# More idle products on TensorE in the front of a fused attention and gated-convolution kernel

## The chip, the cores and the metric

The kernel runs on one core of one Trainium2 chip. A core has five engines that run side by side and meet at semaphores: PE (TensorE, matrix products, with a separate row PEld for the loading of its stationary operand), DVE (VectorE), ACT (ScalarE), POOL (GpSimd) and SP (SyncE, which here only issues transfers). Sixteen DMA engines move data between the memory (HBM) and the core. Each engine works through its instructions strictly in the order in which they were written. The metric is the device time of one execution, in microseconds (us).

## What is computed

The reference is an attention over 8 batches, 12 heads, 448 positions and 64 elements a head, whose softmax has an additional 1 in its denominator, followed by a gated convolution that is done with Fourier transforms:

```python
# attention
scores = scale * np.matmul(q, k.transpose(0, 1, 3, 2))
m = np.max(scores, axis=-1, keepdims=True)
e = np.exp(scores - m)
attn = e / (np.sum(e, axis=-1, keepdims=True) + np.exp(-m) + 1e-09)
attn_out = np.matmul(attn, v)
x = attn_out.transpose(0, 2, 1, 3).reshape(B, S, H * D)
# gated convolution
x1, x2, x3 = split(x @ w_proj, 3)
x2_conv = irfft(rfft(x2, axis=1) * rfft(filter_fft, axis=0), axis=1)
out = (x1 * x2_conv * x3) @ w_out
```

All inputs and the output are float32; the kernel computes in bfloat16 with float32 sums.

## The kernel before

**Attention.** The 96 heads are handled in 48 pairs, six to a batch. For the first two batches (`staged`), k, q and v of each pair are loaded by SP's queue into a staging buffer (L398, L403), cast to bfloat16, nearly all by POOL (k in L425, q in L431, v in L438), turned by PE transposes (L465 and L467 for k, L474 for q, L499 for one piece of the first pair), and copied out of PSUM by DVE or ACT (L482 to L495, L502). For the later batches (`loaded`) the turning is done by DMA transposes on SP's queue (L542, L547). A pair's scores are products of `kT` and `qT` (L773 for three tiles of keys with two heads each, L775 for the shared rest of the keys), the exponentials run on ACT (L780, L786), the products with v on PE (L798, L806), and DVE divides by the sum: `rec` in L819 and L820, the result `xb` in L821. In the first two batches PE turns `xb` (L901), and DVE or ACT copies it to `xT` (L908, L910).

**Convolution.** For each batch DVE folds `xT` (L950, L953, L958), PE multiplies by the weights and by tables of sines (L981, L1011, L1049, L1095, L1134), ACT and DVE do the products between, and PE multiplies by `wout` (L1207); ACT copies the result out (L1219) and SP's queue stores it (L1226). Early on, PE also mirrors the table (L678), turns it (L692) and computes the filter's spectrum (L725, L728).

**The order.** All of it is written as tasks with an engine, an estimated cost and a wanted time. The class `Plan` plays them through on its own estimated clock: at each moment each engine takes the first of its waiting tasks, sorted by wanted time, that is ready. That gives one fixed order for each engine, and also the PSUM bank of each task; there are eight banks. The planned times are estimates and not those of the chip.

**Idle products.** Before any data is there, PE does 38 products of a tile of zeros with itself (`spin`, L1314). When the order is fixed, `fillers` (L232) goes through PE's tasks once more. Wherever there is a planned gap between the planned end of one task and the planned start of the next, and that end lies between the first two numbers of `FILL` (L60), it sets `count` products of the same kind (L1306) ahead of the next task, if `count` is at least 2 and some PSUM bank is unused throughout the planned gap. The third number of `FILL` is the share of the planned gap that `count` is to take, with 0.056 us counted for one product:

```python
if end is not None and self.FILL[0] <= end < self.FILL[1]:
    count = int(self.FILL[2] * (at - end) / 0.056)
```

Their results are never read. The product itself is 128x128 by 128x128 in bfloat16. Because an engine works in order, the task behind them can't start before they have been issued, however early its data is there. A bank that a preceding task used has to be read out first, so the first idle product can carry a wait for the engine that reads it.

Of the kernel before, what the change touches and what calls it, by code (L numbers as in the profile page):

```python
# [41 lines left out]
class Plan:  # L42
# [14 lines left out]

    NBANKS = 8
    LOW = 4
    FILL = (3.0, 36.0, 0.6)  # L60
    PAIRS = ("sc", "op")
    CAP = {"sc": 2, "op": 2, "hy": 5}

# [168 lines left out]
    def fillers(self, order, gone):  # L232
# [7 lines left out]
        for n, (at, t) in enumerate(order):  # L240
            if t[2] != "PE":
                continue
            if end is not None and self.FILL[0] <= end < self.FILL[1]:
                count = int(self.FILL[2] * (at - end) / 0.056)
                free = [
# [1144 lines left out]
```

## Time and profile before

| | |
|---|---|
| median of 4 runs | 382.97 us (382.32 to 384.26) |
| the profiled execution's own time | 382.79 us |
| its span, first to last instruction | 380.9 us |
| PE busy | 365.8 us (96%), 3681 products |
| DVE busy | 258.6 us (68%) |
| ACT busy | 262.1 us (69%) |
| POOL busy | 113.8 us (30%) |
| idle products L1306 | 90, from 5.0 to 34.7 us |
| mean granted clock of PE | 0.995 |

An engine's busy time counts its computing instructions. The granted clock is the share of full speed at which PE was allowed to run. The 40 digits of a row of slices stand for 9.5 us each. A line of the timeline has the start, the length, the engine, the line of the kernel, the operation with its tiles and shape, the number of instructions merged, and in brackets how long the engine had been idle and what ended the wait. Durations of products overlap, since PE is pipelined; the spacing of their starts tells how fast they went.

### The profile page before, as it was taken

How to read it: one execution, taken by the hardware profiler on the slowest of the kernel's cores; microseconds unless marked ns; L12 is line 12 of the kernel's file. 1: busy time of each engine (PE TensorE's matmuls, PEld its weight loads, DVE VectorE, ACT ScalarE, POOL GpSimd, SP SyncE). 2: the span in 40 equal slices, each digit the busy share in tenths (PEclk: the TensorE clock that was granted, in tenths of full speed). 3: DMA queues.
4: the chain of work that ended last, by engine and by line, in shares of the span. 5: the costliest groups of instructions: out<-in, count | busy, mean ns of one | idle time of the engine just before them, and what ended most of it. 6: DMA issues, size and time to landing. Idle time of an engine off the chain costs nothing.

```text
span 380.9 us, 9521 instructions
## 1 busy us (share of the span) xinstructions
PE 365.8 (96%) x3681; PEld 224.6 (59%) x3681; DVE 258.6 (68%) x672; ACT 262.1 (69%) x456; POOL 113.8 (30%) x232
## 2 busy tenths in 40 slices
PE   8887999999999999999999999999999999999994
PEld 7566765556655567555765555655555555655552
DVE  6496769945888548893489845694377936984770
ACT  6686876756886768877787846776778477544622
POOL 4795822422653635453362510000000000000000
PEclk9998999999999999999999999999999999999999
DMA  8999999989999999999999975932422034315205
GB/s 214 252 236 251 234 203 222 132 118 251 192 214 207 182 296 242 223 159 244 268 241 157 228 160 120 202 85 100 98 54 44 18 102 91 84 46 122 83 0 167
DMA packets 148653, 62.27 MB, mean 163 GB/s; under 512 B 113469, under 2 KB 145024, under 8 KB 148608
## 3 DMA queue, kind: packets, MB, share of 16 engines
q1 hardware_dynamic: 111184, 51.89, 61.3%
q0 software_dynamic: 37184, 9.54, 26.7%
q8 instruction: 29, 0.48, 0.5%
q10 hardware_dynamic: 240, 0.23, 0.2%
q14 instruction: 16, 0.13, 0.1%
HBM read 43.86 MB, written 11.01 MB: 144 GB/s over the span
## 4 chain that ended last, share of the span: by engine, by line
PE 66%; DMA 12%; DVE 10%; ACT 4%; POOL 3%; issue 3%; SPq 2%; ACTq 0%; POOLq 0%; DVEq 0%
PE psum L1095 21%; PE psum L1207 11%; PE psum L1011 7%; PE psum L806 6%; PE psum L773 6%; PE psum L981 5%; DMA nat<-in_k_dram 4%; DMA out_dram<-osb 2%; DMA rests<-in_v_dram 2%; PE psum L1049 2%; ACT e L780 2%; DMA nat<-in_q_dram 2%; PE psum L775 2%; DVE t L1063 1%; POOL vn L602 1%
## 5 line engine op out<-in xcount | busy, mean ns | idle before, releaser
L780 ACT ACTIVATE e<-psum 128x896 bf16<-128x896 f32 x144 | 125.6, 923 | 19.3 <-PE psum L773 18.5
L1095 PE MATMUL psum<-xT,wproj_bf 128*128 128x448 bf16 x576 | 121.1, 352 | 1.5 <-DVE g L1110 1.3
L1095 PEld LDWEIGHTS <-wproj_bf 128*128 128x128 bf16 x576 | 54.1, 97 | 46.3 <-issue 3.4
L1207 PE MATMUL psum<-wout_bf,yT 128*128 128x384 bf16 x288 | 51.8, 326 | 0.4 <-DVE g L1110 0.2
L1219 ACT COPY osb<-psum 128x384 f32<-128x384 f32 x56 | 26.0, 484 | 28.1 <-PE psum L1207 24.7
L806 PE MATMUL psum<-vn,e 128*128 128x65 bf16 x1152 | 44.7, 194 | 0.0
L1107 ACT CAST x<-psum 128x448 bf16<-128x448 f32 x48 | 25.8, 537 | 27.5 <-PE psum L1095 27.4
L773 PE MATMUL psum<-qT,kT 64*128 64x448 bf16 x288 | 41.7, 357 | 1.1 <-DVE xb L821 0.6
L1063 DVE TENSOR_TENSOR t<-xs,hrs 113x768 bf16<-113x768 bf16 (+1 forms) x64 | 34.8, 579 | 9.3 <-ACT xs L1057 9.0
L806 PEld LDWEIGHTS <-e 128*128 128x128 bf16 x1152 | 39.0, 98 | 2.7
L602 POOL CAST vn<-nat 128x192 bf16<-128x192 f32 x72 | 28.1, 418 | 41.1 <-DMA nat<-in_v_dram 26.4
L1207 PEld LDWEIGHTS <-yT 128*128 128x128 bf16 x288 | 27.7, 98 | 19.6 <-issue 1.4
L819 DVE TENSOR_SCALAR rec<-psum 128x8 f32<-128x8 f32 x48 | 7.8, 162 | 44.8 <-PE psum L806 39.2
L536 POOL DMA_DIRECT2D nat<-in_q_dram x28 | 24.9, 890 | 40.1 <-DMA qT<-nat 24.9
L1110 DVE TENSOR_TENSOR g<-x,psum 128x448 bf16<-128x448 bf16 x48 | 29.4, 615 | 10.5 <-PE psum L1095 9.9
L981 PE MATMUL psum<-wproj_bf,xf 128*113 128x384 bf16 x192 | 35.2, 327 | 0.0
L821 DVE TENSOR_TENSOR xb<-psum,rec 128x512 bf16<-128x512 f32 x48 | 33.2, 691 | 1.7
L1057 ACT CAST xs<-psum 113x384 bf16<-113x384 f32 (+1 forms) x64 | 27.5, 496 | 4.7 <-PE psum L1049 3.8
L1011 PE MATMUL psum<-xf,wproj_bf 128*128 128x452 bf16 x144 | 30.5, 356 | 0.0
L786 ACT ACTIVATE er<-psum 128x448 bf16<-128x448 f32 x48 | 26.7, 557 | 4.0 <-PE psum L775 4.0
L981 PEld LDWEIGHTS <-xf 128*113 128x113 bf16 x192 | 24.6, 132 | 6.6 <-issue 0.9
L1143 ACT CAST cr<-psum 128x452 bf16<-128x452 f32 x48 | 24.2, 556 | 3.5 <-PE psum L1134 3.5
(113 smaller groups left out, 459.9 us busy)
## 6 DMA issues: line engine op xcount, KB each, us to landing
nat<-in_k_dram SPq DMA_DIRECT2D x48, 192.0 KB, 5.5
nat<-in_v_dram SPq DMA_DIRECT2D x48, 192.0 KB, 5.3
out_dram<-osb SPq DMA_DIRECT2D x24, 384.0 KB, 3.3
nat<-in_q_dram POOLq DMA_DIRECT2D x20, 168.0 KB, 6.9
nat<-in_q_dram SPq DMA_DIRECT2D x11, 224.0 KB, 6.6
wproj_bf<-in_moe_w_proj_dram POOLq DMA_DIRECT2D x2, 1152.0 KB, 15.3
rests<-in_k_dram SPq DMA_DIRECT2D x8, 192.0 KB, 5.5
rests<-in_v_dram SPq DMA_DIRECT2D x8, 192.0 KB, 6.9
```

The costliest lines, as they stand in the source:

```text
L602: nc.gpsimd.tensor_copy(vn[b % 2][:, hp, 4 * u : 4 * u + 3, 0:DH], sv[:, u])
L773: nc.tensor.matmul(sc[:, u, 0:S], kT[b % 2][c, hp, t, :], qT[b % 2][c, hp, :])
L780: nc.scalar.activation(e[:, 0 : 2 * S].rearrange("p (u n) -> p u n", u=2), pair(("sc", ("S", i, t)))[:, :, 0:S], AF.Exp, scale=SCALE,)
L806: nc.tensor.matmul(out_bank(u)[:, n, :], P["e"][1 + t][:, u * S + n * 128 : u * S + n * 128 + 128], vn[b % 2][:, hp, 4 * u + t, :], start= ...
L821: nc.vector.tensor_tensor(W["xb", b][:, hp].rearrange("p n (u d) -> p u n d", u=2), op[:, :, :, 0:DH], rec[:].unsqueeze(3).to_broadcast([1 ...
L981: nc.tensor.matmul(pps[:FQ, :DCH], W["xf", b][:, pg, kt, 0:FQ], wproj_bf[:, kt, D + ch * DCH : D + (ch + 1) * DCH], start=(kt == 0), stop= ...
L1011: nc.tensor.matmul(pps[:, 0 : 4 * FQ], wproj_bf[:, kt, D + dt * 128 : D + (dt + 1) * 128], W["xf", b][:, :, kt, 0:FQ], start=(kt == 0), st ...
L1057: nc.scalar.copy(L["xs", par, ch][:K, pg % 2, :], L["Z", pg, ch][:K, :DCH])
L1063: nc.vector.tensor_tensor(t[:K], L["xs", par, ch][:K], h, op=ALU.mult)
L1095: nc.tensor.matmul(p[:, :S], wproj_bf[:, kt, 2 * part * D + dt * 128 : 2 * part * D + (dt + 1) * 128], xT()[:, kt, 0:S], start=(kt == 0), ...
L1110: nc.vector.tensor_tensor(g[:, dt, :], L["x1", dt], p[:, :S], op=ALU.mult)
L1207: nc.tensor.matmul(ops[:n, :DCH], y[:, dt, 0:n], wout_bf[:, dt, ch * DCH : (ch + 1) * DCH], start=(dt == 0), stop=(dt == NDT - 1),)
```

## The change

One line changes:

```diff
-    FILL = (3.0, 36.0, 0.6)
+    FILL = (3.0, 50.0, 0.9)
```

The idle products take nine tenths of a planned gap instead of six tenths, and planned gaps that begin up to 50 us on the planner's clock are considered instead of 36 us. The order of the tasks and their banks are decided before `fillers` runs and stay as they are. The products are zeros times zeros as before, and their results are still read by nothing.

## The prediction

> **What bounds the kernel now.** I read first the page, for when PE (TensorE) is busy and at what clock:
>
> ```profile
> PE   8887999999999999999999999999999999999994
> ...
> PEclk9998999999999999999999999999999999999999
> ```
>
> A slice is 9.5 us. PE is short of full only in the first four, and in the fourth its clock dips. After 38 us it is full nearly everywhere, so what counts is when PE comes out of the front. Whatever still delays it after its last free wait stands, at first sight, in the end time. Next I cut the front into stretches of 3.41 us that end where the clock changes (columns: stretch, length, busy us of each engine, granted clock, DMA):
>
> ```profile
> 8.37:11.79 3.42, 1.87 (x26) 1.41 (x25) 0.96 (x2) 2.04 (x3) 2.73 (x11) 1.00 1.12 264
> ...
> 28.85:32.26 3.41, 1.48 (x20) 0.93 (x17) 3.10 (x10) 1.42 (x3) 1.79 (x5) 1.00 1.15 241
> 32.26:35.68 3.42, 3.42 (x30) 2.64 (x29) 0.75 (x1) 2.41 (x6) 0.87 (x2) 0.50 1.21 241
> ```
>
> PE was busy 1.48 of 3.41 us, and exactly then the clock fell to 0.50 and stayed there for 3.42 us. In the first row PE was busy 1.87 us and the clock stayed at 1.00. So in this execution the border for keeping the clock lay somewhere between 1.48 and 1.87 busy us in such a stretch. Then the timeline of PE in the front (start, length, line, what, count, idle before and its releaser); L1306 are the idle products:
>
> ```profile
> 10.23 0.37 PE L474 MATMUL psum<-ident_bf,q 112*128 112x112 bf16 x4 [1.28 <-POOL q L431]
> 10.44 0.95 PE L1306 MATMUL psum<-idle 128*128 128x128 bf16 x14
> 11.65 0.36 PE L775 MATMUL psum<-qT,kT 128*128 128x448 bf16 x1 [0.27 <-DVE kT L484]
> ...
> 16.29 0.61 PE L1306 MATMUL psum<-idle 128*128 128x128 bf16 x8
> 16.74 0.35 PE L775 MATMUL psum<-qT,kT 128*128 128x448 bf16 x1
> ...
> 27.22 0.40 PE L901 MATMUL psum<-ident_bf,xb 128*128 128x128 bf16 x4 [1.14 <-DVE xb L821]
> ...
> 32.05 0.45 PE L901 MATMUL psum<-ident_bf,xb 128*128 128x128 bf16 x4 [1.93 <-DVE xb L821]
> 32.29 1.70 PE L1306 MATMUL psum<-idle 128*128 128x128 bf16 x14
> 33.78 0.58 PE L775 MATMUL psum<-qT,kT 128*128 128x448 bf16 x1
> 34.16 0.95 PE L1306 MATMUL psum<-idle 128*128 128x128 bf16 x7
> 35.04 0.84 PE L773 MATMUL psum<-qT,kT 64*128 64x448 bf16 x4
> ```
>
> One product's record is 0.22 us long at full clock and 0.31 at half. So 14 in 0.95 us are (0.95 - 0.22)/13 = 0.056 us apart, and 14 in 1.70 us (1.70 - 0.31)/13 = 0.107. The waits in brackets are the cushions of the front; the last are 1.14 us at 27.22 and 1.93 us at 32.05. Last I read the chain that ended last:
>
> ```profile
> 31.30 0.70 DVE xb L821
> ...
> 131.53 4.89 DMA out_dram<-osb
> ...
> 136.44 0.49 ACT osb L1219
> ```
>
> VectorE (DVE) ends both of PE's long waits (its xb at 31.30 is in the chain, the one at 26.47 too), and after 32.05 us PE, idle products included, is the chain. Much later, from 87 to 137 us, it runs through SP's queue and transfers.
>
> **The change part by part.** The built program has 145 idle products in the front instead of 90, 55 more; every other engine's order is unchanged. By place (time in the profile before, count before to after): 5.0 us 6 to 9; 5.7 us 2 to 3; 6.0 us 16 to 24; 7.5 us 2 to 4; 7.75 us 4 to 7; 8.5 us 0 to 2; 10.4 us 14 to 22; 16.3 us 8 to 12; 22.9 us 8 to 12; 23.8 us 0 to 2; 25.6 us 6 to 9; 29.8 us 3 to 5; 32.3 us 14 to 21; 34.2 us 7 to 11; 39.7 us 0 to 2. Only the last place comes from the longer front.
>
> - Up to 8.6 us: 19 more, 19 x 0.056 = 1.06 us. The next real work is the transpose at 10.23, which waits for POOL's cast of q, and that for a load; 1.28 us were idle there. The two products at 8.5 us newly wait for the exponential that frees their bank, which ended at 8.35 us and will end some 0.7 later, at 9.0; four transposes queued behind them then end near 9.8. Cost 0; with the cover gone it would be 1.06 us.
> - 10.4 us: 22 x 0.056 = 1.23, so they end at 11.67 where the scores L775 began at 11.65 behind a copy on DVE. Cost 0.02, gone in the 0.43 us that PE waits at 12.67 for POOL. Taken as 0.
> - 16.3 us: 4 x 0.056 = 0.22 us. The scores at 16.74 followed the products directly, and the products with v, L806, behind them end 0.22 later. DVE had idled 1.57 us until 18.47 for exactly those, and from there it works almost without a break to the two xb of the chain. So DVE hands 0.21 us to PE at 27.22 and 32.05. This is the one early group that isn't covered. Bounds 0 (DVE's small idle times take it) and 0.22; I take 0.21.
> - 22.9, 23.8 and 25.6 us: 9 more, 0.50 us, inside the 1.14 us before 27.22. Cost 0. 29.8 us: 2 more, 0.11, inside the 1.93 us. Cost 0.
> - 32.3 and 34.2 us: here no cushion is left, and the clock decides. The first product starts at 32.29 + 0.21 = 32.50. If the clock falls at 32.26 as before: 21 x 0.107 = 2.24, scores L775 at 34.74 (before: 33.78); 0.37 for them; from 35.11 five products at 0.107 up to 35.68, six at 0.056, and 0.07 to the scores L773: 36.05 (before: 35.04). These four now run at full clock, 0.39 us (12.97 to 13.36 in the timeline) in place of 0.68, so what follows starts at 36.44 against 35.72: +0.72. If the clock doesn't fall: 32.50 + 21 x 0.056 = 33.68; the copy of kT that L775 needs, ended by ACT at 33.55, comes 0.21 later; L775 at 33.82, products from 34.01, 11 x 0.056 + 0.07, L773 at 34.70, the next at 35.09: -0.63.
> - 39.7 us: 2 x 0.056 = 0.11, of which PE had about 0.09 free there (0.25 us between two steps that are 0.16 apart elsewhere); their bank is freed by ACT's L735, long done. +0.02, with 0.11 as the upper bound.
>
> Does the clock still fall? With two more products behind 30.0 us, and both ends 0.21 later, the idle stretch is 1.82 us in place of 1.93. Busy time in the stretch of 3.41 us before the fall goes from 1.48 to about 1.59, against the border between 1.48 and 1.87. It is nearer to the row that fell, so I take the fall as before.
>
> The Trainium skill, in "TensorE: Matmul & The Clock Gate" (Part 1 and the closing table), asks only that PE have no idle gap above about 3 us between bursts. The row differs: here the clock fell after 1.93 us of idleness. By the page no gap of this front needs products, the clock would hold with and without the change, and its cost would be that of the uncovered products alone: about +0.4, the 0.21 carried over and 4 x 0.056 at 34.2 us.
>
> **The sum.** +0.72 + 0.02 (and up to 0.1 more at the two changes of pace), taken as +0.8 on the profiled execution. That took 382.79 us (span 380.9, 1.9 around it), 0.18 below the median of the four runs, 382.97. 382.79 + 0.8 = 383.6.
>
> **The rivals.**
> 1. The clock stays full: -0.63 + 0.02 at 36 us. For it: 1.59 busy us isn't far from 1.87, and nothing shows that the stretches begin at the same moment in each run. Against it: 1.59 is nearer to 1.48. Not all of it reaches the end: at 136.97 PE waits 0.43 us for ACT, which waits for a store to land, in the chain through the transfers. If that is pinned, 0 is left; if it follows, -0.61; I take -0.4: 382.4.
> 2. Slower by more than 0.5%: the delay costs a place on SP's queue. The chain enters SP's queue at 87.67 behind an ACT copy that PE releases, so +0.8 enters with it; if a load or store then stands behind one DMA transpose more, that adds its issue, 1.88 us for the one at 128.23. 382.79 + 0.8 + 1.9 = 385.5. It decides once 1.1 us or more is added to the 0.8. For it: hardly any slack in that stage, POOL's casts of q waiting for PE at 37.41. Against it: the queues' order is fixed, and PE's own waits there are short.
> 3. Faster by more than 0.5%: the clock stays full and the stage from 87 to 137 us follows wholly, its waits at 114.37 (0.83) and 136.97 (0.43) going too: -0.61 - 1.26 = -1.9, 380.9. Against it: nothing in the change touches what these waits end on.
> 4. It does nothing: every extra product lies in idle time, 382.8. The lines after 32.05 speak against it, where the products are the chain.
>
> **How the numbers follow.** Half a per cent, 1.9 us, is about what a measurement of this kernel can tell from no change; the four runs alone reach from 382.32 to 384.26. Chances: the fall as before 0.40 (383.6, its own range 382.6 to 384.6); clock full 0.18 (382.4); nothing 0.05 (382.8); a place lost 0.25 (385.5); faster 0.12 (380.9). The first three are within half a per cent: 0.63. The range 381.0 to 385.8 leaves out half of the faster case and about a third of the slower.
>
> **What would show it.** Right: 145 products; PE's wait before 10.23 nearly gone; DVE's L819 at 18.47 later by 0.2; L901 at about 32.25; a granted clock of 0.5 behind it; 21 products 0.107 apart; the real work after L773 later by 0.7 to 0.9 us, kept to the end. Wrong: no fall of the clock (then 0.6 earlier at 36 us), a second fall elsewhere (up to half of 3.4 us), or a shift that grows between 87 and 137 us.

## The result and the profile after

The changed kernel takes 382.68 us (median of 43 executions, 380.27 to 391.67), the kernel before 384.05 us (64 executions, 381.80 to 388.39). The ratio is 0.9951, with a 95% interval from 0.9932 to 0.9970: half a per cent faster, just inside what I had called no change (0.5%), and in the opposite direction to my +0.2%. The ratio leaves out executions more than 1.5% above the fastest of their kernel, 12 of the 43 of the changed kernel (a group of their own, from 387.4 to 391.7 us) and 4 of the 64 of the kernel before, so it compares the lower group of the one with nearly all executions of the other; over all executions the two kernels have nearly the same mean, 384.29 and 384.50 us.

The profiled execution took 381.92 us with a span of 380.1 us (before 382.79 and 380.9). First the page's rows of slices of the changed kernel, PE's busy share and its granted clock, and the shares of the chain that ended last:

```profile
PE   8988999999999999999999999999999999999994
...
PEclk9998999999999999999999999999999999999998
...
PE 79%; DVE 11%; DMA 3%; ACT 2%; issue 1%; SPq 1%; POOL 1%; ACTq 0%; POOLq 0%; DVEq 0%
```

The last of these rows in the kernel before:

```profile
PE 66%; DMA 12%; DVE 10%; ACT 4%; POOL 3%; issue 3%; SPq 2%; ACTq 0%; POOLq 0%; DVEq 0%
```

The front is a little fuller, the dip of the clock in the fourth slice is still there, and transfers (DMA) have 3% of the chain, where they had 12% before. The stretches of 3.41 us on either side of the fall of the clock:

```profile
29.19:32.60 3.41, 1.59 (x22) 1.20 (x21) 2.54 (x10) 1.63 (x3) 1.22 (x4) 1.00 1.16 244
32.60:36.02 3.42, 3.42 (x31) 2.73 (x30) 1.84 (x2) 2.02 (x5) 2.04 (x3) 0.50 1.22 241
```

PE was busy 1.59 of 3.41 us, and the clock fell to 0.50 for 3.42 us, as forecast. PE's timeline in the front:

```profile
9.96 0.36 PE L474 MATMUL psum<-ident_bf,q 112*128 112x112 bf16 x4
10.15 1.39 PE L1306 MATMUL psum<-idle 128*128 128x128 bf16 x22
11.38 0.35 PE L775 MATMUL psum<-qT,kT 128*128 128x448 bf16 x1
...
15.39 0.83 PE L1306 MATMUL psum<-idle 128*128 128x128 bf16 x12
16.07 0.35 PE L775 MATMUL psum<-qT,kT 128*128 128x448 bf16 x1
...
19.49 0.37 PE L474 MATMUL psum<-ident_bf,q 112*128 112x112 bf16 x4 [0.98 <-POOL q L431]
...
31.82 0.40 PE L901 MATMUL psum<-ident_bf,xb 128*128 128x128 bf16 x4 [1.82 <-DVE xb L821]
32.05 1.94 PE L1306 MATMUL psum<-idle 128*128 128x128 bf16 x21
33.79 0.58 PE L775 MATMUL psum<-qT,kT 128*128 128x448 bf16 x1
34.16 1.38 PE L1306 MATMUL psum<-idle 128*128 128x128 bf16 x11
35.47 0.80 PE L773 MATMUL psum<-qT,kT 64*128 64x448 bf16 x4
36.11 0.28 PE L798 MATMUL psum<-vn,er 64*128 64x65 bf16 x8
```

The 55 additional products are all there, and the wait of 1.28 us in front of 10.23 is gone. The products with v (L798) that begin at 36.11 began at 35.72 before: PE is 0.39 us later here, and 0.41 us at 45 us. At the end it is 0.8 us *earlier*. So 1.2 us went between 45 us and the end. Most of it went at the two waits that rival 3 named. PE's timeline of the kernel before has them so, the second for a copy by ACT (L1219) whose own line follows:

```profile
114.37 1.29 PE L1095 MATMUL psum<-xT,wproj_bf 128*128 128x448 bf16 x6 [0.83 <-DVE g L1110]
...
136.97 0.35 PE L773 MATMUL psum<-qT,kT 64*128 64x448 bf16 x1 [0.43 <-ACT osb L1219]
```

```profile
136.44 0.48 ACT L1219 COPY osb<-psum 128x384 f32<-128x384 f32 x1 [1.64 <-DMA out_dram<-osb]
```

The same in the changed kernel:

```profile
114.09 1.29 PE L1095 MATMUL psum<-xT,wproj_bf 128*128 128x448 bf16 x6
...
134.65 1.14 PE L981 MATMUL psum<-wproj_bf,xf 128*113 128x384 bf16 x6
135.71 0.70 PE L773 MATMUL psum<-qT,kT 64*128 64x448 bf16 x4
```

```profile
135.54 0.48 ACT L1219 COPY osb<-psum 128x384 f32<-128x384 f32 x1 [1.01 <-DMA out_dram<-osb]
```

ACT's copy (L1219) still waits, 1.01 us instead of 1.64, for a store of an output tile to land, because the pool `otp` has three buffers and the copy needs the oldest. But PE's four scores at 135.71 run without a break, where before the fourth of them waited 0.43 us; and the wait of 0.83 us at 114.37 is gone too. PE gains 0.69 and 0.63 us at these two places; behind them it gains 0.71 more up to 200.82, where a wait of 0.56 us for DVE goes, and loses 0.84 from there to 206.98.

### The profile page after: what moved, and what is told of

The parts are those of the page before. It is cut to its first block, busy times and chain, and to the rows that moved or that the text cites. A ratio compares the mean times of both kernels' runs of the same rounds, so it can differ in the third digit from the quotient of the medians.

```text
span 380.1 us, 9631 instructions
## 1 busy us (share of the span) xinstructions
PE 367.9 (97%) x3736; PEld 227.9 (60%) x3736; DVE 257.8 (68%) x672; ACT 262.6 (69%) x456; POOL 112.0 (29%) x232
## 4 chain that ended last, share of the span: by engine, by line
PE 79%; DVE 11%; DMA 3%; ACT 2%; issue 1%; SPq 1%; POOL 1%; ACTq 0%; POOLq 0%; DVEq 0%
PE psum L1095 25%; PE psum L1207 14%; PE psum L806 8%; PE psum L981 8%; PE psum L1011 7%; PE psum L773 7%; PE psum L1049 2%; PE psum L775 2%; DMA rests<-in_v_dram 2%; PE psum L1134 2%; DVE g L1110 1%; DVE t L1063 1%; DMA nat<-in_q_dram 1%; DVE xf L958 1%; DVE xb L821 1%
## 5 line engine op out<-in xcount | busy, mean ns | idle before, releaser
L1219 ACT COPY osb<-psum 128x384 f32<-128x384 f32 x56 | 26.1, 484 | 27.1 <-PE psum L1207 25.7
L602 POOL CAST vn<-nat 128x192 bf16<-128x192 f32 x72 | 27.2, 407 | 37.4 <-DMA nat<-in_v_dram 27.4
```

Source lines behind the costliest of these rows:

```text
L602: nc.gpsimd.tensor_copy(vn[b % 2][:, hp, 4 * u : 4 * u + 3, 0:DH], sv[:, u])
```

## The experiments

In all of them, "later" and "earlier" are PE's moments in the profiled execution against the profile before, at the same instruction. The time "from 45 us to the end" is how much PE lost (+) or gained (-) behind 45 us of the profile before. Each median is of 12 executions if nothing else is said. The kernel before, run again on each occasion, had medians of 384.61, 384.42, 384.52, 385.22 and 384.64 us.

**Which group of products matters?** Four kernels leave out or keep one group of the products each. `FILL` takes several stretches for this:

```diff
-            if end is not None and self.FILL[0] <= end < self.FILL[1]:
-                count = int(self.FILL[2] * (at - end) / 0.056)
+            share = 0.0 if end is None else sum(s for a, z, s in self.FILL if a <= end < z)
+            if share:
+                count = int(share * (at - end) / 0.056)
```

No products at all behind the first 38:

```diff
-    FILL = (3.0, 36.0, 0.6)
+    FILL = ((3.0, 3.1, 0.0),)
```

> No idle products behind the first 38 (0 in place of 90). Clock theory (the products pay because they keep the granted clock from falling behind PE's waits): more falls of the clock between 8 and 40 us, each worth 0.7 to 1.7 us, so 1 to 4 us slower than before (0.3 to 1%). Cost theory (a product in front of work that is ready only delays it; this was the prediction's sum): the 21 products behind 32 us, 0.107 us each at half clock, go, up to 2 us faster at 36 us, less what the fall costs. Transfer theory (the products move the times at which casts free staging room, and the gain arises in the loads up to 140 us): PE leaves the front within 0.5 us of before, and the difference arises later.

Measured: ratio 0.999 (0.9946 to 1.0033), median 386.44 us (381.61 to 390.32), 6 of 12 executions above 386.5 us.

The larger share before a planned 16 us only:

```diff
-    FILL = (3.0, 36.0, 0.6)
+    FILL = ((3.0, 16.0, 0.9), (16.0, 36.0, 0.6))
```

> Nine tenths only in planned gaps that begin before 16 us (27 of the 55 added products, at 5 to 12 us), six tenths behind that. Clock theory: the clock held in this stretch in both profiles, so at most a small part of the change's gain, 0 to 0.7 us. Transfer theory: most of the change's gain of 1.9 us (0.5%), since the first scores and turns are what moved by a microsecond. Cost theory: no difference, the idle time before 10 us covers it.

Measured: 0.9984 (0.9949 to 1.0019), 384.14 us (381.06 to 386.37).

The larger share from a planned 30 us only:

```diff
-    FILL = (3.0, 36.0, 0.6)
+    FILL = ((3.0, 30.0, 0.6), (30.0, 50.0, 0.9))
```

> Nine tenths only in planned gaps that begin behind 30 us (15 of the 55: 3 to 5 at 30 us, 14 to 21 and 7 to 11 at 32 to 35, 0 to 2 at 40). Cost theory: 0.5 to 0.7 us slower than before. Clock theory: if the gain comes from the stretch where the profiles show the fall, most of 1.9 us faster, with the fall at 32 us gone in part of the executions. Transfer theory: 0.5 us slower, as by cost.

Measured: 0.9972 (0.9939 to 1.0005), 384.14 us (381.74 to 385.93).

The larger share up to a planned 31 us and no products behind it, so none where the clock falls:

```diff
-    FILL = (3.0, 36.0, 0.6)
+    FILL = ((3.0, 31.0, 0.9),)
```

> The change without its products behind 32 us: nine tenths up to planned 31 us, none from there on (32 fewer than the change at 32 to 35 us, 2 fewer at 40). Cost theory: PE leaves this place 1 to 1.4 us sooner than with the change, so about 1 us faster than it, 2.5 to 3 us (0.7%) faster than before. Clock theory: the time is that of the change or up to 1 us slower, since PE then idles in place of the products until its data comes and the clock may stay low for a second stretch of 3.4 us.

Measured: 0.9943 (0.9907 to 0.9979), 383.62 us (380.97 to 387.81).

No kernel of the four stands clearly apart from the others: the intervals overlap. What the profiles show is more useful. In the fourth, the scores at 33.16 are 1.88 us ahead of those of the kernel before at 35.04, as no product stands in front of them. But without these products PE is idle again, and the clock stays low for two stretches in a row:

```profile
28.57:31.98 3.41, 1.63 (x19) 0.90 (x16) 2.48 (x10) 1.74 (x3) 1.28 (x3) 1.00 1.16 258
31.98:35.40 3.42, 2.73 (x35) 1.82 (x36) 2.14 (x2) 3.39 (x7) 1.99 (x4) 0.50 1.22 235
35.40:38.80 3.40, 3.40 (x23) 2.67 (x21) 1.92 (x5) 1.38 (x4) 2.79 (x6) 0.50 1.15 281
```

At 45 us it is 0.34 us behind. From 32 us to there it lost 1.23 us and the changed kernel 0.63, so in these executions the products at 32 and 34 us earned more than they cost, with the clock back one stretch earlier. And all four profiles lose time where the changed kernel had gained it: from 45 us to the end +5.02, +3.70, +1.16 and +1.90 us. PE's wait for ACT's copy near 137 us is 3.57, 1.63, 1.30 and 2.49 us in them. The chain names the store behind it, with its issue and the time until it landed (131.53 and 4.89 in the profile before); in the first, the second and the third kernel:

```profile
133.94 7.05 DMA out_dram<-osb
```

```profile
132.14 4.98 DMA out_dram<-osb
```

```profile
132.62 4.89 DMA out_dram<-osb
```

So the wait has two sources: in the first kernel the store took 2.16 us longer to land, in the other two it took no longer than before but was issued 0.61 and 1.09 us later, with PE 0.50 us earlier and 0.22 us later than before at 134 us. My theory had no such term. New theory: the time is decided by how long ACT waits for the output buffer, and that has little to do with the products.

**Take that wait away.** A fourth output buffer; the order on each engine stays the same:

```diff
-    otp = ctx.enter_context(tc.tile_pool(name="otp", bufs=3))
+    otp = ctx.enter_context(tc.tile_pool(name="otp", bufs=4))
```

In the kernel before, twice:

> The kernel before with four output buffers osb in place of three; every engine's order is the same, so only ACT's wait for a store to land (which holds PE between 136 and 141 us, 0.4 to 3.6 us in the profiles so far) can go. Store theory (this wait is where executions differ, and the front's products move the end only through it): 1 to 2 us faster than before, executions closer together, and no clock fall near 140 us. Front theory (the end follows what the front does, the wait only passes it on): within 0.5 us of before. If 140 us is limited by the kT transposes on the same queue: the wait stays under another name, no gain.

> The kernel before with four output buffers again. Store theory: 0.996 of before again, no execution above 386.5.

Measured: 0.9962 (0.9933 to 0.9991), 383.17 us (381.53 to 385.53), and 0.9927 (0.9893 to 0.9961), 382.79 us (379.88 to 384.12).

In the changed kernel, twice:

> The changed kernel with four output buffers. Store theory: the same time as the kernel before with four buffers, within 0.4 us, plus the +0.4 us that PE is later at 36 us in the profile of the changed kernel. Front theory: still 1.5 to 2 us faster than the kernel before with four buffers.

> The changed kernel with four output buffers again. Store theory: within 0.6 us of the kernel before with four buffers on the same occasion, no execution above 386.5. If the front's products have a gain of their own: 1.5 to 2 us below it.

Measured: 0.9958 (0.9926 to 0.9990), 382.67 us (379.44 to 385.33), and 0.9966 (0.9933 to 1.0000), 382.99 us (380.44 to 385.99).

And with the fourth kernel above (no products behind a planned 31 us):

> Nine tenths up to planned 31 us, no products behind it, and four output buffers. In its profile without the fourth buffer PE was 1.9 us ahead of before at 35 to 110 us and waited 2.5 us at 139. Store theory: that lead comes through, 1.5 to 2 us faster than the kernel before with four buffers, 380 us. Front theory: as without the fourth buffer, 0.994 of before.

Measured: 0.9969 (0.9938 to 0.9999), 382.61 us (381.22 to 386.52). Here the expectation, 380 us, missed: it counted on a lead of PE from 35 to 110 us, but the lead at 33.16 us had turned into 0.34 us of lateness by 45 us, and with four buffers PE was 0.62 us late there.

With four buffers the kernel before and the changed one cannot be told apart: means of 24 executions each of 382.93 and 382.86 us, 0.07 apart. PE's wait for ACT's copy near 137 us is gone in every profile with four buffers; of the changed kernel's second run PE's timeline there reads:

```profile
134.52 0.55 PE L773 MATMUL psum<-qT,kT 64*128 64x448 bf16 x4
134.91 0.28 PE L798 MATMUL psum<-vn,er 64*128 64x65 bf16 x8
```

**How repeatable is the result itself?** The changed kernel and the kernel before, unchanged:

> The changed kernel again, beside the two kernels with four buffers. By the first measurement 0.995 of before (0.993 to 0.997). Store theory: the profile has either no wait at 137 us and a time near 381.5, or a wait of 2 us or more and a time above 384.

> The changed kernel a third time. If the change is really faster: 0.995 of before (0.993 to 0.997), as at first. If its share of executions with the long wait near 137 us differs from one occasion to the next: anything from 0.993 to 1.007, with executions near 381.5 and near 388.

> The kernel before, unchanged, measured as if it were another kernel: what this measurement makes of no change at all. Store theory (the end differs between executions of one kernel by the wait for a store near 137 us and a clock fall that follows it): a ratio anywhere from 0.995 to 1.005, as wide as the change's own. Front theory: 1.000 within 0.002.

Measured: the changed kernel 0.9996 (0.9944 to 1.0048), 387.09 us (380.62 to 390.33), and 1.0032 (0.9987 to 1.0078), 388.12 us (382.75 to 391.41); the kernel before 1.0006 (0.9972 to 1.0040), 384.85 us (383.33 to 387.57). The gain of half a per cent did not come back. Three occasions gave the same program 0.9951, 0.9996 and 1.0032, and in the last two 7 and 9 of 12 executions were above 386.5 us. Over all their executions the means of these two are 386.59 and 387.90 us, against 384.71 and 384.90 us of the kernel before on the same occasions. In its second profile the changed kernel waited 1.82 us near 137 us and took 386.14 us, just between the two cases expected of it. The ratio of the kernel before to itself, 1.0006, fits both expectations; what separates them is its profile.

The profile of the *unchanged* kernel shows what differs from one execution to the next. First ACT and PE near 136 us, then the store in the chain:

```profile
136.15 0.48 ACT L1219 COPY osb<-psum 128x384 f32<-128x384 f32 x1 [2.98 <-DMA out_dram<-osb]
```

```profile
136.68 0.35 PE L773 MATMUL psum<-qT,kT 64*128 64x448 bf16 x1 [1.78 <-ACT osb L1219]
```

```profile
129.35 6.77 DMA out_dram<-osb
```

Same program as the profile before, but the store took 6.77 us instead of 4.89 and PE waited 1.78 us instead of 0.43. What follows costs once more. The stretches of 3.41 us of this execution, first in the front, then around the wait:

```profile
28.43:31.84 3.41, 1.86 (x32) 1.31 (x29) 3.04 (x12) 1.78 (x3) 1.81 (x5) 1.00 1.16 262
31.84:35.26 3.42, 3.09 (x63) 2.49 (x61) 1.97 (x2) 3.19 (x7) 1.93 (x3) 1.00 1.21 233
...
134.26:137.67 3.41, 1.63 (x32) 1.04 (x32) 0.00 (x0) 1.52 (x3) 0.94 (x1) 1.00 1.16 382
137.67:141.08 3.41, 3.41 (x21) 2.43 (x18) 1.59 (x4) 1.49 (x3) 2.14 (x6) 0.50 1.20 316
```

In the front the clock did not fall here: the stretches begin elsewhere in this execution, the last one before 32 us held 1.86 busy us instead of 1.48, and PE was 1.54 us earlier at 36.8 us than in the profile before, 0.45 of it already at 32 us, with nothing in the program changed. At 137.67, after 1.63 busy us, it fell, which took PE from 0.30 us earlier (137.1 us) to 1.35 later (145 us). In the third execution of the changed kernel it is the same with larger numbers; its chain and PE's timeline:

```profile
132.70 8.40 DMA out_dram<-osb
141.12 0.49 ACT osb L1219
```

```profile
141.65 0.53 PE L773 MATMUL psum<-qT,kT 64*128 64x448 bf16 x1 [5.15 <-ACT osb L1219]
```

So one wait, for one store, makes 0 to 5.15 us in executions of one kernel, and the fall of the clock behind it up to 1.7 us more. With the fourth buffer no profile has either, and the upper group of times goes too: above 386.5 us were 28 of 67 executions of the changed kernel and 50 of 227 of the kernel before with three buffers, and 2 of 96 with four (shares of 0, 0.6, 0.9 and 1.2).

**How much lateness of the front reaches the end?** Four buffers, without products (twice), with twice the share, and with a share between:

```diff
-    FILL = (3.0, 36.0, 0.6)
+    FILL = (3.0, 50.0, 1.8)
```

> No idle products behind the first 38, with four output buffers. Without the fourth buffer PE was 1.5 us later than before at 45 us in its profile (the clock stood at 0.5 for 10 us of the front) and the end 6.5 later. Sum theory (what PE loses in the front reaches the end, the rest is the store): 1 to 2 us slower than the kernel before with four buffers, about 384.3, no execution above 387.5. If the transfers up to 140 us hold PE anyway: the same as the kernel before with four buffers, 382.9.

> No idle products behind the first 38, four output buffers, once more. Theory (carried to the end): whatever PE is late at 45 us in the profiled execution, the end is later by that less 0.6 to 1.2 us; the executions scatter by 4 us or more, because the clock falls once or twice in the front in some of them; median 382.8 us within 0.8. Rival (taken up by the transfers): the end stays within 1 us of that of the other profiles with four buffers although PE is 1 us or more later or earlier than theirs at 45 us.

> Twice the change's share (1.8 of the planned gaps, 303 products in place of 145), with four output buffers. Sum theory: the 28 and 15 products more than before at 32 and 34 us are no longer covered, 43 x 0.056 to 0.107 = 2.4 to 4.6 us, and part of those before 10 us carry over too: 2.5 to 5 us slower than the kernel before with four buffers, 385.5 to 388. If the transfers hold PE anyway: less than 1 us slower.

> Share 1.2 with four output buffers: 197 idle products, 52 more than the changed kernel. Theory (with a fourth buffer what PE loses in the front is carried to the end, and the scatter of the executions, 379.4 to 386.0 us with shares of 0.6 and 0.9, is that of the granted clock in the front, which falls in some executions): PE is busy enough here that the clock no longer falls, so the highest and the lowest of the executions lie within 2.5 us, as they did with share 1.8 (386.69 to 388.35), around a median of 383 to 385 us; in the profile no stretch at 0.5 behind 9 us, and the end against the end of the profile before is later by what PE is late at 45 us less 0.6 to 1.2 us. Rival (the transfers between 87 and 137 us take up the first 2 us of what PE is late): the median is that of the other kernels with four buffers, 382.6 to 383.2 us, with their scatter of 4 us or more.

Measured: without products 0.9959 (0.9927 to 0.9992), 382.80 us (381.01 to 385.54), and 0.9963 (0.9923 to 1.0003), 383.47 us (381.75 to 387.97). Share 1.8: 1.0068 (1.0040 to 1.0095), 387.05 us (386.69 to 388.35). Share 1.2: 0.9967 (0.9935 to 1.0000), 383.74 us (381.92 to 385.55). The median without products, 382.80, is what the rival expected (382.9) and not the sum theory (384.3), so the medians alone don't decide; the profiles do.

All profiles with four buffers side by side:

| kernel with four buffers | later at 45 us | later at the end | from 45 us to the end |
|---|---|---|---|
| before (share 0.6), first | -1.32 | +0.37 | +1.69 |
| before (share 0.6), second | -1.58 | -2.81 | -1.23 |
| changed (0.9), first | -0.52 | -1.13 | -0.61 |
| changed (0.9), second | -0.80 | -1.56 | -0.76 |
| 0.9, none behind 31 us | +0.62 | -0.43 | -1.05 |
| no products, first | +2.08 | +1.39 | -0.69 |
| no products, second | +0.71 | +0.05 | -0.66 |
| share 1.2 | +0.04 | -0.07 | -0.11 |
| share 1.8 | +5.19 | +4.25 | -0.94 |

Except for the first line, the last column lies between -0.11 and -1.23 us, whether PE comes out of the front 1.58 us early or 5.19 us late. In the first line PE waited more for DVE: 0.92, 1.16, 1.01 and 0.95 us at 102, 114, 171 and 201 us, in place of 0.15, 0.83, 0.20 and 0.56 in the profile before. With a share of 1.2 the gain of 0.11 us is less than the 0.6 to 1.2 us expected. So without the wait for the store the front's lateness does go on to the end, but for what such waits for DVE add; the rival, that the transfers between 87 and 137 us take up the first 2 us of it, falls. What is gained behind 45 us is the wait near 137 us of the profile before (0.43), and part of the other at 114.37 (0.83). What PE is late at 45 us, however, is as much the execution's as the kernel's: it differs by 1.4 us between the two executions without products, and by 0.3 us between those of each other pair. In the first one without products the clock was low in the front for long, which cost it the lead that the missing products gave:

```profile
32.00:36.00 4.00, 2.52 (x20) 1.05 (x19) 2.41 (x4) 3.42 (x7) 1.66 (x3) 0.50 1.22 242
36.00:40.00 4.00, 4.00 (x41) 3.39 (x40) 2.49 (x6) 2.13 (x4) 2.53 (x5) 0.50 1.15 289
40.00:44.00 4.00, 4.00 (x32) 2.81 (x31) 1.69 (x5) 3.74 (x10) 2.92 (x7) 0.93 1.13 231
```

With a share of 1.8 the clock stays full, but the products themselves are the work; PE's timeline:

```profile
36.25 2.51 PE L1306 MATMUL psum<-idle 128*128 128x128 bf16 x42
38.59 0.35 PE L775 MATMUL psum<-qT,kT 128*128 128x448 bf16 x1
38.78 1.39 PE L1306 MATMUL psum<-idle 128*128 128x128 bf16 x22
40.11 0.55 PE L773 MATMUL psum<-qT,kT 64*128 64x448 bf16 x4
```

The expectation that the clock of the front alone makes the scatter with four buffers did not hold: with a share of 1.2 the profile has no fall of the clock in the front, and the executions still scatter over 3.6 us, where 2.5 at most was expected. Why those with a share of 1.8 lie within 1.7 us I can't say.

Nor is the clock itself settled by PE's busy time. With four buffers the changed kernel (first) kept its clock after 1.61 busy us in a stretch, and the kernel without products behind 31 us lost it after 1.91; the stretch and the next one in each:

```profile
30.51:33.92 3.41, 1.61 (x28) 1.44 (x27) 1.83 (x8) 1.65 (x4) 1.25 (x3) 1.00 1.18 249
33.92:37.33 3.41, 3.41 (x62) 2.86 (x62) 2.61 (x5) 3.08 (x6) 2.29 (x3) 1.00 1.21 252
```

```profile
32.05:35.47 3.42, 1.91 (x31) 1.16 (x32) 2.19 (x4) 2.55 (x6) 1.37 (x3) 1.00 1.22 236
35.47:38.88 3.41, 3.41 (x31) 2.80 (x28) 2.20 (x6) 2.30 (x4) 2.68 (x5) 0.50 1.16 264
```

It fell after 1.73 and 2.02 too (the two profiles without products, four buffers) and held after 1.74 (the larger share from 30 us only). So between 1.6 and about 2 busy us both happen, and what decides there stays open.

**Does a later front make the wait for the store longer?** The share of 1.8 with three buffers, six executions:

> Share 1.8 with the three output buffers of the kernel before: 303 idle products, PE some 5 us late at 45 us. Theory (the stores that hold the third buffer land at times of their own, set by the queues; a later PE waits less for them): the wait of PE for ACT's copy at about 136 to 141 us is below 0.5 us in the profile, few executions or none are more than 3 us above the lowest, median 386.5 to 388 us. Rival (the stores are issued behind work that PE releases, so a later front makes them land later by as much, and more idle products bring the long waits more often): a third or more of the executions lie above 390 us, and the profile shows a wait of 1 us or more there.

Measured: 1.0150 (1.0095 to 1.0205), 390.63 us (388.93 to 394.16), 5 of 6 executions above 390 us: the rival's expectation. Having only three buffers costs 3.6 us here (387.05 with four, on another occasion; the ratios differ by 0.8%). In the profile PE is 5.76 us later at 45 us, and the store lands later with it, at 143.33 us instead of 136.42; its chain and PE's timeline:

```profile
135.33 8.00 DMA out_dram<-osb
```

```profile
143.88 0.35 PE L773 MATMUL psum<-qT,kT 64*128 64x448 bf16 x1 [2.33 <-ACT osb L1219]
```

So the store is not pinned to a time of its own; a later PE doesn't get rid of the wait.

## Why the prediction was right or wrong

- **Up to 8.6 us and at 10.4 us: right.** The real work behind all 19 products, at 8.62 us, came 1.17 us later (9.79); 1.06 was summed, and the clock's first rise was 0.34 us later in this execution. The wait of 1.28 us before 10.23 took all of it up, and the scores behind the 22 products at 10.4 us even began 0.27 us earlier (11.38).
- **16.3 us: the step right, its way to the end not.** The twelve products take 0.22 us more (0.83 against 0.61), as worked out. But I let DVE carry 0.21 us to PE at 27.22 and 32.05, and in this execution L901 began at 31.82, 0.23 earlier. PE had 0.98 us to wait at 19.49 for POOL's q, and in four further profiles with these twelve products (the changed kernel's second and third, and both with four buffers) PE was at 32 us 0.50, 0.44 and 0.33 later and 0.22 earlier. The term lay within its bounds (0 and 0.22) and is smaller than what one execution differs from the next.
- **32.3 and 34.2 us: the fall right, the sum near by luck.** The clock fell after 1.59 busy us and 1.82 us of idleness, as worked out, and the next stretch was full again. From 32 to 36.8 us PE lost 0.61 us; I had 0.51. But the terms were others: the fall came at 32.60 us, 0.55 us behind the first of the 21 products, and not ahead of it, so only about half of them went through at half pace (their mean spacing is (1.94 - 0.31)/20 = 0.08 us). Up to the scores L775 that cost 0.25 us where I had 0.75; from there to L798 it cost 0.38 us, with the clock low up to 36.02, where I had a gain of 0.24.
- **39.7 us: right**, +0.02.
- **"Does the clock still fall?" had no one answer.** Near 32 us it fell in the profiled executions before and after and in the second of the changed kernel, and not in the second profile of the kernel before, nor in the third of the changed one. Each time the clock changes at a multiple of 3.41 us after its first rise, and that rise came anywhere from 4.28 to 6.62 us in these executions. The border holds in these profiles: the clock fell after 1.48, 1.59 and 1.63 busy us in a stretch, and held after 1.86, 1.87 and 2.09. In the profiles of the other kernels, shown above, it isn't sharp: between 1.6 and about 2 busy us both happen. The Trainium skill says in "TensorE: Matmul & The Clock Gate" (Part 1) that this window is free-running and doesn't start with the kernel. The moments of the first rise agree, and I should have drawn the conclusion: a profile shows one position of the windows, and the price of the products is a mean over all of them. The page's closing table asks for no idle gap above about 3 us. Keeping to that was not enough here: the clock fell with PE idle for 1.8 to 1.9 of 3.41 us.
- **The step that failed is the last of the sum, "+0.8 on the profiled execution"**, which takes everything from 45 us on as it was, because "nothing in the change touches what these waits end on". The shift was +0.41 us at 45 us, and the rest of the kernel then changed by -1.20 us in this profile, +2.34 and +7.13 us in the two other profiles of the changed kernel, and +3.65 us in the second of the kernel before. This term, which I had at 0, is larger than every term that I worked out. It isn't the change's: it moved by 3.65 us with nothing changed. Most of it is the output buffer's wait with the fall of the clock behind it, and one profile before couldn't show its scatter; the four times, 382.32 to 384.26 us, didn't either.
- **The rivals.** Rival 3 named the place; but it tied the two waits to a clock that stays full, and they went although the clock fell. That its price for them, 1.26 us, is near the 1.20 is partly luck: the gains there were 0.69 and 0.63, and the rest up to the end nearly cancels. Rival 2 expected a loss in the same stage, by a place on SP's queue; executions of 387 us and more exist, through the wait for the store. A store issued later on that queue was part of it in two profiles (0.61 and 1.09 us), but the change isn't needed for it. Rival 4, that the products do nothing, is what four buffers show on average: 0.07 us between shares of 0.6 and 0.9. The condition for that, as I read it, is that the products lie in idle time or pay by the clock; with the share of 1.8 they do neither, and PE is 5.19 us late at 45 us.

So the measured 0.9951 is no gain of the products that these runs could confirm. Two things stay open about the long executions: why one store takes 4.89 us to land in one execution and 8.40 in another, and is issued later in some, and why the executions with a long time were more frequent with the changed kernel (28 of 67 against 50 of 227); PE at 45 us was 0.41 and 1.13 later and 0.41 earlier in its three profiles, 1.54 earlier in the second of the kernel before, too few to tell whether a later front brings them.

A version that beats both: the kernel before with a fourth output buffer, 0.9962 and 0.9927 of the kernel before. Over all executions its means were 383.19 and 382.67 us; the changed kernel with three buffers had 384.29, 386.59 and 387.90. Whether the products are worth keeping these runs can't tell: with four buffers the mean without any is 383.49 us, 0.6 us above the others, in a scatter of 4 us and more.

## What to carry to other kernels

Before summing shifts of a few tenths in the front, look for a wait on a transfer further back, above all one for a buffer of a small pool: if it sits in the chain, its scatter can decide the time, and one more buffer was worth more here than the front. Run the unchanged kernel against itself and compare two of its profiles; what differs there is no effect of a change. Price a step that hangs on TensorE's clock as a mean over where the 3.41 us stretches can begin, not at the one place that a profile shows.

## What was not expected of the hardware

- With three buffers the store of the same output tile took from 4.89 to 8.40 us from issue to landing, in executions of programs whose order on every queue is the same.
- The stretches of the granted clock, 3.41 us each, begin at another moment in each execution (first rise at 4.28 to 6.62 us), so the same program meets a fall of the clock in one execution and not in the next; the two profiles of the kernel before differ by 1.54 us at 36.8 us, 1.09 of it from between 32 and 36.8 us, where one of them has the fall.
- In five of eight profiles with a wait of PE of more than 1 us near 137 us, a stretch at half clock followed it, which added 1.3 to 1.7 us.
